# Reordering the first layer's small matmul groups, and moving one M quarter to an earlier step, in a cross-attention and leaky-ReLU layer kernel on one core

## The chip, the core and the metric

The kernel runs on one core of one Trainium2 chip. The metric is the device time of one execution in microseconds (us), as the median of some runs. The engines are TensorE (PE in the profile; PEld are its weight loads), VectorE (DVE), ScalarE (ACT), GpSimd (POOL) and SyncE (SP, which here only issues DMAs). Matmuls accumulate in PSUM, which has eight banks; VectorE and ScalarE carry ("evict") the results to SBUF.

## The reference

```python
def _attn_ref(x, state):                      # x (8, 8, 512, 64), state (8, 8, 32, 64)
    scores = scale * np.matmul(x, state.transpose(0, 1, 3, 2))
    a = np.exp(scores - scores.max(-1, keepdims=True))
    a /= a.sum(-1, keepdims=True) + 1e-09
    xread = np.matmul(a, state)
...
    sread = np.matmul(a2, x)                  # a2: the same with state and x exchanged
    return np.concatenate([xread, sread], axis=2)
def _moe_ref(x, w_in, w_out):                 # (4352, 512) @ (512, 2048), @ (2048, 512)
    h = x @ w_in
    return np.maximum(0.01 * h, h) @ w_out
```

Each of 8 batches has 8 heads, 512 tokens and 32 state rows per head. The heads' results stand side by side as 512 features; two layers with a leaky ReLU between them follow.

## The kernel before, in words

**How the work is cut.** The read of the state is folded into the first layer: for each batch the kernel makes M = state times w_in (256 rows of heads and state, in two groups of 128, by 2048), so that the first layer is probabilities times M. M is made in four quarters of 512 columns. `a_m(a, c, tag)` (line 413) makes quarter c of a batch with eight small matmuls (line 425) that use 64 rows and 32 columns of the array each, into two banks of the pool `tag`; `m_evict` (433) carries it to SBUF with the engine that it is given. A stretch in which TensorE makes such small matmuls, between full ones of 128 by 128, is called a session here. `a_scores` (line 260 of the trace) makes a batch's scores with eight small matmuls of the same form. Both may stand in one session.

**PSUM.** There are pools of banks by name: "sc" and "big" (one tile of two banks each), "py" and "ph" (two tiles of one bank each). A tile of a pool can be taken again when its last readers are done.

**The order is written by hand.** Each engine runs its instructions in the order in which the program emits them. Nothing is sorted by a planner, so where a line stands in the program is its place in its engine's queue.

**The stretch of the change.** Batch 0 (object `a0`) starts with attention of its own: after the exponentials, `recip0` (871) makes reciprocals on VectorE, `recip0_rows` (877, matmuls on line 824) spreads them over the rows by 16 small matmuls for each of two groups u, and `probs0` (881) multiplies on VectorE into `a0.aT`. Around these stand M's quarter 0 and 1 of batch 0 and quarter 0 of batch 1 (`a1`). Then batch 0's first layer runs in pairs of 128-wide blocks: `open_ff1_0` takes two banks, `ff1_0` (matmuls on line 960) adds the two groups g, `relu0` (972 for a tile of two banks, 968 for two of one) writes `h0` on ScalarE. Quarters 2 and 3 of batch 0 are evicted in halves (`m_halves`, 983 and 985) by VectorE between the pairs.

The second layer of batch 0 is done in pieces: `piece(b, hT, i, jq)` (545, matmuls on line 551) adds four of the sixteen blocks to the output of row block i; `jq` from 0 to 3 are its steps, and `js` takes half of one. Row blocks 0 and 1 use "py" banks, 2 and 3 the tile `wide` of "big". Between the pieces stand batch 1's transposes (1027) of its input, which GpSimd's queue loads into `x1` (889) in two halves and VectorE casts (1007), batch 1's scores, and M's quarter 2 of batch 1. ScalarE's exponential of batch 1 (`a_exp`, 288) follows VectorE's maximum, spread and difference (270, 278, 284).

Then batch 1's first layer runs in 16 steps `s` (`ff1`, 443: two matmuls on line 446 and one activation on line 451 into alternate "ph" banks). With it go the rest of batch 0's pieces and, from `s == 4` on, batch 2's scores (`a2`), for which the transposed state is made by GpSimd (213) and a DMA transpose of SyncE's queue (218). Batch 2's differences and exponentials go in halves (284, 334), and a second exponential over columns (351) follows. The later batches go in the same manner, with products of sums and differences in the second layer; they are not touched.

Of the kernel before, what the change touches and what calls it, by code (L numbers as in the profile page):

```python
# [27 lines left out]
def kernel(  # L28
# [24 lines left out]
    VEC, SCA, POO = nc.vector.tensor_copy, nc.scalar.copy, nc.gpsimd.tensor_copy  # L53
# [195 lines left out]
    def st_of(a, g, k):  # L249
        rows = slice(D * g, D * (g + 1))  # L250
        if a.b == 0:
            return stbd[rows, k, g ^ (k // 2), :]
        t = st1 if a.b == 1 else st_t[0][:, a.b - 2] if a.b < 4 else st_t[1][:, a.b - 4]
        return t[rows, NS * k:NS * (k + 1)]
# [31 lines left out]
    def block_exp(sh, n):  # L286
        e1 = att.tile([P, n * NS], BF16, name="e1", tag="e1", bufs=1)
        nc.scalar.activation(out=e1[:], in_=sh[:], func=AF.Exp)
        return e1
# [21 lines left out]
    def a_max(a):  # L311
        a.flat = a.sc[:].rearrange("p g c -> p (g c)")
        a.m1 = block_max(a.flat, NB)
# [9 lines left out]
    def a_exp(a):  # L323
        a.e1 = block_exp(a.sh, NB)
# [18 lines left out]
    def a_max2(a):  # L343
        a.m2 = att.tile([P, 2], FP32, name="mcol", tag="mcol")
        nc.vector.tensor_reduce(out=a.m2[:], in_=a.sc[:], axis=AX.X, op=ALU.max, negate=True)  # L345
# [67 lines left out]
    def a_m(a, c, tag):  # L413
        if not hasattr(a, "M"):
            a.M = mpool.tile([P, 2, DFF], BF16, name="M", tag="M")
        if tag in ("ph", "py", "phpy"):
            pm = [psum.tile([P, DM], FP32, name="pm", tag=t) for t in (tag[:2], tag[-2:])]
            at = [t[:] for t in pm]
        else:
            pm = psum.tile([P, 2, DM], FP32, name="pm", tag=tag, bufs=1)  # L420
            at = [pm[:, g, :] for g in range(2)]
        for k in range(NK):
            for g in range(2):
                v, r = (k // 2, 2 * (k % 2) + (g ^ (k // 2))) if a.b == 0 else (g, k)
                nc.tensor.matmul(  # L425
                    at[v][NS * r:NS * (r + 1)],
                    lhsT=st_of(a, g, k),
                    rhs=w_in_bf[D * g:D * (g + 1), k, DM * c:DM * (c + 1)],
                    start=True, stop=True,
                )  # L430
        return pm

    def m_evict(a, c, pm, copy):
        cols = slice(DM * c, DM * (c + 1))
        if isinstance(pm, list):
            for g in range(2):
                copy(a.M[:, g, cols], pm[g][:])
        else:
            copy(a.M[:, :, cols], pm[:])  # L439
# [105 lines left out]
    def piece(b, hT, i, jq, bank=None, copy=SCA, js=range(4)):  # L545
        if jq == 0 and js[0] == 0:
            y = ys[b, i] = Y()
            y.py = psum.tile([P, DM], FP32, name="py", tag="py")[:] if bank is None else bank
        y = ys[b, i]
        for j in [4 * jq + v for v in js]:  # L550
            nc.tensor.matmul(  # L551
                y.py, lhsT=hT[:, j, P * i:P * (i + 1)], rhs=w_out_bf[:, j, :],
                start=(j == 0), stop=(j == 15),
            )
        if jq == 3 and copy is not None:
            y_store(b, i, copy)

    def y_store(b, i, copy):
        tag = ("ysb", "s1", "ysb", "s6")[i]
        ysb = ypool.tile([P, DM], FP32, name="ysb", tag=tag, bufs=3 if tag == "ysb" else 1)  # L560
        copy(ysb[:], ys[b, i].py)
        nc.sync.dma_start(rows_of(b)[i], ysb[:])
# [213 lines left out]
    a0, a1, a2 = att_of[:3]  # L776
# [43 lines left out]
    def spread0(dst, parts, start):  # L820
        for i, part in enumerate(parts):
            for t in range(NT):
                for c in range(NK):
                    nc.tensor.matmul(
                        dst[NS * c:NS * (c + 1), P * t:P * (t + 1)],
                        lhsT=part[:, NK * t + c:NK * t + c + 1].to_broadcast([P, NS]),
                        rhs=ident[:], start=start, stop=start or (t == NT - 1 and i == 1),
                    )
# [42 lines left out]
    def recip0(u):  # L871
        q = att.tile([P, NG], BF16, name="q0", tag="q0")
        with nc.allow_low_precision(reason="one rounding, of the finished reciprocal"):
            nc.vector.reciprocal(q[:], r0[u][:])
        return q

    def recip0_rows(u, q):
        qb0[u] = psum.tile([P, S], FP32, name="qb0", tag="ph")
        spread0(qb0[u], (q,), True)

    def probs0(u):
        nc.vector.tensor_tensor(out=a0.aT[:, u], in0=e10[u][:], in1=qb0[u][:], op=ALU.mult)
# [52 lines left out]
    q = [recip0(0)]  # L935
    pm = a_m(a0, 0, "sc")
# [1 line left out]
        SCA(a0.M[:, g, :DM], pm[:, g, :])  # L938
    sum0(1)
    q.append(recip0(1))  # L940
    for u in range(2):
        recip0_rows(u, q[u])
        probs0(u)
    m_evict(a1, 0, a_m(a1, 0, "py"), SCA)
    m_evict(a0, 1, a_m(a0, 1, "big"), VEC)

    h0 = hpool.tile([P, 16, S], BF16, name="hT", tag="hT")

    def open_ff1_0(tag):
        if tag in ("sc", "big"):
            pr = psum.tile([P, 2, S], FP32, name="php", tag=tag, bufs=1)
            return pr, [pr[:, 0], pr[:, 1]]
        ph = [psum.tile([P, S], FP32, name="ph", tag=tag) for _ in range(2)]
        return ph, [p[:] for p in ph]

    def ff1_0(banks, j, g, vs=(0, 1)):
        for v in vs:
            nc.tensor.matmul(  # L960
                banks[v], lhsT=a0.M[:, g, P * (j + v):P * (j + v + 1)], rhs=a0.aT[:, g, :],
                start=(g == 0), stop=(g == 1),
            )
# [22 lines left out]

    t0, b0 = open_ff1_0("sc")
    t2, b2 = open_ff1_0("py")
    for t, j in ((b0, 0), (b2, 2)):
        for g in range(2):  # L990
            ff1_0(t, j, g)
    relu0(t0, 0)
    relu0(t2, 2)
    m_evict(a1, 1, a_m(a1, 1, "big"), VEC)
    for j, tag in ((4, "ph"), (6, "big"), (8, "py"), (10, "big"), (12, "py"), (14, "ph")):
        t, bk = open_ff1_0(tag)
        for g in range(2):
            ff1_0(bk, j, g)
        relu0(t, j)
        if j == 4:  # L1000
            m_halves(a0, 2, "sc")
        elif j == 8:
            a_scores(a0)
            m_halves(a0, 3, "ph")
            a_max2(a0)
# [9 lines left out]
        a_exp2(a0, g)  # L1015
    wide = psum.tile([P, 2, DM], FP32, name="pyw", tag="big", bufs=1)
    half = (range(0, 2), range(2, 4))
    for u in range(2):
        piece(0, h0, 2 + u, 0, bank=wide[:, u], js=half[0])
    for i in (0, 1):  # L1020
        piece(0, h0, i, 0, js=half[0])
    for u in range(2):
        ps = psum.tile([P, NT, 2, P], BF16, name="pxt2", tag="ph")
        for t in range(NT):
# [19 lines left out]
        tw_sum(1, j, j + 2, nc.gpsimd)  # L1044
    for i in (0, 1):
        piece(0, h0, i, 1)
    a_exp(a1)
    for i in (2, 3):
        piece(0, h0, i, 1)
# [28 lines left out]
    for s in range(16):  # L1078
        ff1(a1, h1, s)
        if s in (1, 3):  # L1080
            two = ((2, SCA), (3, VEC)) if s == 1 else ((0, SCA), (1, SCA))
            for i, copy in two:
                piece(0, h0, i, 3, copy=None, js=half[1])
            for i, copy in two:
                y_store(0, i, copy)
        elif s % 2:
            piece(*fill[s // 2 - 2])
        if s == 4:
            a_scores(a2)
            pm = a_m(a1, 3, "big")  # L1090
            a_max(a2)
            a_diff_halves(a2)
            a_max2(a2)
        elif s == 5:
            m_evict(a1, 3, pm, SCA)
            load_state(1)
        elif s == 7:
            a_exp_half(a2, 0)
            a_open(att_of[3], 3)
            a_xt_dma(att_of[3])  # L1100
        elif s in (9, 11):
            if s == 9:
                a_exp_half(a2, 1)
            a_exp2(a2, s // 2 - 4)
            if s == 9:
                a_a2t_pair(0, (0,))
                a_recip(a2)
                a_probs(a2)
            else:
                a_probs2(a2)  # L1110
                load_x(4, nc.sync)
        elif s == 13:
            a_probs2(a1)
            a_a2t_pair(0, (1,))
            pm = [a_m(a2, 0, "big"), a_m(a2, 1, "sc")]
            m_evict(a2, 0, pm[0], SCA)
            m_evict(a2, 1, pm[1], VEC)
            q1 = two_open(h1, 2 * P, ("S0", "S1"), "py")
            for n in (1, 2, 3):
                two_sum(q1, n, 0, 4, nc.vector)  # L1120
            two_sum(q1, 3, 4, 8, nc.vector)
# [19 lines left out]
    for b in range(2, B):  # L1141
# [22 lines left out]
        for s in range(16):  # L1164
            ff1(a, hT, s)
            if mid and s == (1 if b == 2 else 2):
                (o, c, tag), (o2, c2, tag2) = mid
                pm = a_m(att_of[o], c, tag)
# [71 lines left out]
            if b == 7 and s in FA_AT:  # L1240
                i = FA_AT.index(s)
# [24 lines left out]
    for c in range(2):  # L1266
# [15 lines left out]
        if c == 0:  # L1282
            y_pair(b, 0, 0, HN)
            q = two_open(hs, 0, None, "ph")
# [6 lines left out]
    for n in (1, 2, 6, 5, 7, 3, 4):  # L1291
        two_product(q, n)
        if n in (3, 4):
            u = n - 3
# [43 lines left out]
```

## Time and profile before

| | |
|---|---|
| median of 3 runs | 202.36 us (202.3 to 202.41) |
| the profiled execution's own time | 202.85 us |
| its span, from the first to the last instruction | 201.1 us |
| TensorE's mean granted clock | 1.000 |
| ScalarE's busy time in 24.0 to 30.0 us, and in 42.0 to 49.0 | 1.36 of 6.00, and 6.69 of 7.00 |
| DMA bytes moved in all | 27.75 MB |

A row of the timeline gives start and duration in us, engine, line, operation, what is written from what, shapes and how many instructions are merged; in brackets stand the idle time of the engine before it and what ended it. A merged row's duration runs to the end of its last instruction; matmuls are pipelined, so the next row starts before that end, and the distance between starts is what TensorE pays. In the chain of work that ended last a row gives start, duration, and what.

### The profile page before, as it was taken

The page shows a single profiled execution, that of the slowest core. Times are in us where ns is not written, and L with a number is a line of the kernel's source. Part 1 is how long each engine was busy: PE and PEld are TensorE (multiplying, and loading weights), DVE is VectorE, ACT ScalarE, POOL GpSimd, SP SyncE. Part 2 cuts the span into 40 slices and gives each one's busy share as a digit, 9 for nine tenths or more (in the row PEclk, how much of TensorE's full clock was granted, in tenths as well). Part 3 has the DMA queues.
Part 4 walks back from the last instruction along what each step waited for, and adds up shares of the span by engine and source line. Part 5 has one row for each costly group of instructions (what it writes and reads, how often), then busy time and mean ns, then how long its engine had stood idle before and what let it go on. Part 6 is the DMA issues. An engine that isn't in the chain of part 4 may idle for free.

```text
span 201.1 us, 4627 instructions
## 1 busy us (share of the span) xinstructions
PE 195.6 (97%) x1880; PEld 129.9 (65%) x1880; DVE 160.5 (80%) x241; ACT 141.5 (70%) x273; POOL 72.6 (36%) x77
## 2 busy tenths in 40 slices
PE   7989999999999999999999999999999999999993
PEld 2633544343476767776776677676767777799982
DVE  2767799598999989985999889898999945984712
ACT  3678825999889868766887779777868555757420
POOL 8734164993091373037300770054004600540000
PEclk9999999999999999999999999999999999999999
DMA  6999998597999954852473405220025202210115
GB/s 190 215 206 299 212 290 137 121 307 191 210 194 250 316 53 69 242 215 55 86 227 134 133 14 94 104 109 0 0 103 158 55 3 104 108 49 8 52 38 170
DMA packets 38774, 27.75 MB, mean 138 GB/s; under 512 B 24417, under 2 KB 35809, under 8 KB 38753
## 3 DMA queue, kind: packets, MB, share of 16 engines
q1 hardware_dynamic: 33584, 20.78, 39.2%
q0 software_dynamic: 4832, 6.29, 15.3%
q10 hardware_dynamic: 336, 0.39, 0.9%
q8 instruction: 14, 0.23, 0.5%
q14 instruction: 8, 0.06, 0.1%
HBM read 17.30 MB, written 8.91 MB: 130 GB/s over the span
## 4 chain that ended last, share of the span: by engine, by line
PE 85%; DMA 9%; POOL 3%; ACTq 1%; ACT 0%; DVE 0%; issue 0%; POOLq 0%
PE ph L446 24%; PE ppx L646 18%; PE ppb L646 15%; DMA x<-in_x_dram 8%; PE py L551 7%; PE ppr L703 6%; PE pm L425 3%; PE pf L524 3%; PE pyw L551 3%; PE ppw L646 3%; PE psr L398 2%; POOL w_in_bf L149 2%; PE sc L260 1%; DMA out_dram<-ysb 1%; ACTq L1297 1%; POOL x L889 0%
## 5 line engine op out<-in xcount | busy, mean ns | idle before, releaser
L451 ACT ACTIVATE hT<-ph 128x512 bf16<-128x512 f32 x112 | 66.7, 605 | 24.8 <-PE ph L446 24.0
L446 PE MATMUL ph<-aT,M 128*128 128x512 bf16 x224 | 65.4, 379 | 0.0
L611 POOL TENSOR_TENSOR S<-hT,S 128x512 bf16<-128x512 bf16 x24 | 32.1, 1358 | 82.2 <-DVE S L611 55.5
L646 PEld LDWEIGHTS <-S 128*128 128x128 bf16 x384 | 37.0, 98 | 12.7 <-issue 0.9
L646 PEld LDWEIGHTS <-hT 128*128 128x128 bf16 x288 | 28.0, 98 | 11.1
L611 DVE TENSOR_TENSOR S<-hT 128x1024 bf16<-128x1024 bf16 x24 | 25.0, 1070 | 3.3 <-ACT hT L451 3.3
L446 PEld LDWEIGHTS <-M 128*128 128x128 bf16 x224 | 20.9, 98 | 8.8 <-issue 2.9
L646 PE MATMUL ppx<-tw,S 128*128 128x256 bf16 x160 | 20.8, 273 | 0.0
L551 PEld LDWEIGHTS <-hT 128*128 128x128 bf16 x96 | 9.2, 98 | 11.4 <-issue 0.9
L551 PE MATMUL py<-w_out_bf,hT 128*128 128x512 bf16 x64 | 16.0, 379 | 0.0
L743 DVE TENSOR_TENSOR ysb<-ppb,s 128x512 f32<-128x512 f32 x12 | 8.3, 691 | 6.2 <-PE ppb L646 6.1
L646 PE MATMUL ppb<-w_out_bf,hT 128*128 128x256 bf16 x96 | 12.4, 273 | 0.0
L646 PE MATMUL ppb<-tw,S 128*128 128x256 bf16 x96 | 12.4, 273 | 0.0
L646 PE MATMUL ppb<-w_out_bf,S 128*128 128x256 bf16 x96 | 12.3, 273 | 0.0
L439 ACT CAST M<-pm 128x1024 bf16<-128x1024 f32 x11 | 11.2, 1017 | 0.3 <-PE pm L425 0.3
L646 PE MATMUL ppx<-w_out_bf,hT 128*128 128x256 bf16 x80 | 11.2, 273 | 0.0
L351 ACT ACTIVATE e<-sc,mcol 128x512 bf16<-128x512 f32 x16 | 11.1, 700 | 0.0
L646 PE MATMUL ppx<-tw,hT 128*128 128x256 bf16 x80 | 10.4, 273 | 0.0
L270 DVE TRANSPOSE_TENSOR_REDUCE mrow<-sc 128x32 f32<-128x1024 f32 x7 | 8.7, 1242 | 1.3 <-PE sc L260 1.3
L345 DVE TENSOR_REDUCE mcol<-sc 128x2 f32<-128x1024 f32 x8 | 9.7, 1214 | 0.0
L439 DVE CAST M<-pm 128x1024 bf16<-128x1024 f32 x7 | 8.5, 1217 | 1.4 <-PE pm L425 1.4
L136 POOL CAST xb<-xl 128x2048 bf16<-128x2048 f32 x5 | 9.5, 1895 | 0.0
(153 smaller groups left out, 322.7 us busy)
## 6 DMA issues: line engine op xcount, KB each, us to landing
out_dram<-ysb SPq DMA_DIRECT2D x11, 512.0 KB, 2.7
xl<-in_x_dram SPq DMA_DIRECT2D x5, 1024.0 KB, 6.3
out_dram<-ysb SPq DMA_DIRECT2D x9, 256.0 KB, 4.5
w_in_bf<-in_moe_w_in_dram POOLq DMA_DIRECT2D x4, 512.0 KB, 9.7
xf<-in_x_dram SPq DMA_DIRECT2D x4, 256.0 KB, 3.8
w_out_bf<-in_moe_w_out_dram POOLq DMA_DIRECT2D x4, 256.0 KB, 14.1
x<-in_x_dram POOLq DMA_DIRECT2D x2, 512.0 KB, 15.5
w_out_bf<-in_moe_w_out_dram POOLq DMA_DIRECT2D x2, 512.0 KB, 16.8
```

Source lines behind the costliest of these rows:

```text
L136: nc.gpsimd.tensor_copy(xt[b][:].rearrange("p t h d -> p h t d"), xl[b][:].rearrange("p h (t d) -> p h t d", t=NT),)
L270: nc.vector.tensor_reduce(out=m1[:], in_=flat.rearrange("p (c j) -> p c j", j=NS), axis=AX.X, op=ALU.max, apply_transpose=True,)
L345: nc.vector.tensor_reduce(out=a.m2[:], in_=a.sc[:], axis=AX.X, op=ALU.max, negate=True)
L351: nc.scalar.activation(out=a.e2[:, g], in_=a.sc[:, g, :], func=AF.Exp, bias=a.m2[:, g:g + 1], accum_out=a.r2[:, g:g + 1],)
L439: copy(a.M[:, :, cols], pm[:])
L446: nc.tensor.matmul(ph[:], lhsT=a.M[:, g, P * j:P * (j + 1)], rhs=a.aT[:, g, :], start=(g == 0), stop=(g == 1),)
L451: nc.scalar.activation(out=hT[:, j, :], in_=ph[:], func=AF.Prelu, scale=1 / SCALE, alpha=0.01)
L551: nc.tensor.matmul(y.py, lhsT=hT[:, j, P * i:P * (i + 1)], rhs=w_out_bf[:, j, :], start=(j == 0), stop=(j == 15),)
L611: eng.tensor_tensor(out=part(n), in0=in0, in1=in1, op=op)
L646: nc.tensor.matmul(q[bank][v], lhsT=lhsT, rhs=w_of(n, j), start=q["open", bank] and j == 0, stop=j == 7, skip_group_check=True,)
L703: nc.tensor.matmul(q.bank[w], lhsT=lhsT, rhs=w_of(n, j), start=n in (1, 2, 5) and j == 0, stop=j == HJ - 1, skip_group_check=True,)
L743: nc.vector.tensor_tensor(out=to, in0=of, in1=in1, op=ALU.add)
```

## The change

Four things are moved. M's quarter 0 of batch 1 goes between the two groups' spreads. Quarter 1 of batch 0 goes between the first two groups of the first layer's first pair. The pairs 6 to 12 of batch 0's first layer exchange "big" and "py", and the wide pieces of the second layer's first half step go behind the narrow ones. Last, M's quarter 3 of batch 1 leaves step 4 of batch 1's first layer, where it followed batch 2's scores in "big" banks and was evicted at step 5 by one copy, and goes into batch 0's second layer, between the pieces of step 1 (`jq` = 1) of row blocks 0 and 1 and those of 2 and 3, in "ph" banks, evicted by two copies of ScalarE ahead of batch 1's exponential.

```diff
@@ -938,11 +938,11 @@
-    for u in range(2):
-        recip0_rows(u, q[u])
-        probs0(u)
+    recip0_rows(0, q[0])
+    probs0(0)
     m_evict(a1, 0, a_m(a1, 0, "py"), SCA)
-    m_evict(a0, 1, a_m(a0, 1, "big"), VEC)
+    recip0_rows(1, q[1])
+    probs0(1)
@@ -986,13 +986,15 @@
     t0, b0 = open_ff1_0("sc")
     t2, b2 = open_ff1_0("py")
-    for t, j in ((b0, 0), (b2, 2)):
-        for g in range(2):
-            ff1_0(t, j, g)
+    ff1_0(b0, 0, 0)
+    m_evict(a0, 1, a_m(a0, 1, "big"), VEC)
+    ff1_0(b0, 0, 1)
+    for g in range(2):
+        ff1_0(b2, 2, g)
     relu0(t0, 0)
     relu0(t2, 2)
     m_evict(a1, 1, a_m(a1, 1, "big"), VEC)
-    for j, tag in ((4, "ph"), (6, "big"), (8, "py"), (10, "big"), (12, "py"), (14, "ph")):
+    for j, tag in ((4, "ph"), (6, "py"), (8, "big"), (10, "py"), (12, "big"), (14, "ph")):
@@ -1015,10 +1017,10 @@
+    for i in (0, 1):
+        piece(0, h0, i, 0, js=half[0])
     for u in range(2):
         piece(0, h0, 2 + u, 0, bank=wide[:, u], js=half[0])
-    for i in (0, 1):
-        piece(0, h0, i, 0, js=half[0])
@@ -1044,6 +1046,7 @@
     for i in (0, 1):
         piece(0, h0, i, 1)
+    m_evict(a1, 3, a_m(a1, 3, "ph"), SCA)
     a_exp(a1)
     for i in (2, 3):
         piece(0, h0, i, 1)
@@ -1087,12 +1090,10 @@
         if s == 4:
             a_scores(a2)
-            pm = a_m(a1, 3, "big")
             a_max(a2)
             a_diff_halves(a2)
             a_max2(a2)
         elif s == 5:
-            m_evict(a1, 3, pm, SCA)
             load_state(1)
```

## The prediction

> **What bounds the kernel now.** I read the page first, then the chain of work that ended last, then the timeline of each engine from 10 to 50 us, where all edits lie.
>
> ```profile
> span 201.1 us, 4627 instructions
> PE 195.6 (97%) x1880; PEld 129.9 (65%) x1880; DVE 160.5 (80%) x241; ACT 141.5 (70%) x273; POOL 72.6 (36%) x77
> ```
>
> TensorE is the bound: nearly every 0.1 us that it gains or loses for good is in the time. But the chain says that one stretch isn't its own: the chain leaves TensorE at 24.00 us and goes to a transfer.
>
> ```profile
> 7.48 15.74 DMA x<-in_x_dram
> 23.25 0.69 DVE xb L1007
> ...
> 23.25 0.69 DVE L1007 CAST xb<-x 128x1024 bf16<-128x1024 f32 x1 [0.65 <-DMA x<-in_x_dram]
> ...
> 23.23 0.61 PE L1027 MATMUL pxt<-ident,xb 128*128 128x128 bf16 x8
> 24.00 0.62 PE L1027 MATMUL pxt<-ident,xb 128*128 128x128 bf16 x8 [0.16 <-DVE stf L1011]
> ```
>
> The second half of batch 1's input lands at 23.22. VectorE had idled 0.65 us for it, casts it (0.69), and only then can TensorE make the second group of transposes, at 24.00, after 0.16 us of idling. (The memset named as releaser stands right behind the cast.) So TensorE's work before 24.00 is covered by a transfer already, by a margin of 0.16 us. That decides what the first two hunks are worth.
>
> **The first part (before 24.00).** It adds and removes no arithmetic; it changes the order.
>
> ```profile
> 11.53 0.41 PE L425 MATMUL pm<-w_in_bf,st 64*32 64x512 bf16 x8
> 12.59 0.41 PE L425 MATMUL pm<-w_in_bf,stbd 64*32 64x512 bf16 x8 [0.66 <-DMA w_in_bf<-in_moe_w_in_dram]
> ...
> 13.81 1.03 PE L960 MATMUL ph<-aT,M 128*128 128x512 bf16 x4
> 14.77 0.41 PE L425 MATMUL pm<-w_in_bf,st 64*32 64x512 bf16 x8
> 15.11 1.04 PE L960 MATMUL ph<-aT,M 128*128 128x512 bf16 x4
> 16.07 0.41 PE L425 MATMUL pm<-w_in_bf,stbd 64*32 64x512 bf16 x8
> 16.52 1.02 PE L960 MATMUL php<-aT,M 128*128 128x512 bf16 x4
> 17.38 1.03 PE L960 MATMUL ph<-aT,M 128*128 128x512 bf16 x4
> ...
> 13.07 1.23 DVE L439 CAST M<-pm 128x1024 bf16<-128x1024 f32 x1 [0.48 <-PE pm L425]
> 15.25 1.22 DVE L439 CAST M<-pm 128x1024 bf16<-128x1024 f32 x1 [0.95 <-PE pm L425]
> 16.56 1.29 DVE L985 CAST M<-pm 128x512 bf16<-128x512 f32 x2
> ```
>
> Before, TensorE waits 0.66 us for w_in's second quarter (until 12.59), then does the M group and eight first-layer matmuls. After, the second row of spreads and two first-layer matmuls lie ahead of that wait and fill it, so six are left behind it. Four take 17.38 - 16.52 = 0.86, so two are worth 0.43. The next M group (14.77) needs VectorE's eviction, 13.07 + 1.23 = 14.30, and so goes at about 14.36: 0.41 earlier. The swap of "big" and "py" for pairs 6 to 12 takes away the 0.11 at 16.52 (there the bank waits for the eviction that ends at 15.25 + 1.22 = 16.47), but at 17.38 the matmuls need the halves that VectorE begins at 16.56, and VectorE itself is only 0.41 earlier. So TensorE gets to the transposes **0.41 us earlier**, and then idles 0.16 + 0.41 = 0.57 for the same transfer: worth nothing by this trace (bounds: 0 and -0.41). No step here changes a DMA or its queue: loads of GpSimd's queue keep their order, and SyncE's first state load still follows the cast. The order of the wide and the narrow pieces changes only TensorE's order inside the covered stretch.
>
> **The second part (after 24.00): M's last quarter of batch 1.** Before, it shares a session of small matmuls with batch 2's scores in step 4; after, it has one alone, at about 28.6. First what a session costs.
>
> ```profile
> 18.34 0.41 PE L260 MATMUL sc<-xT,stbd 64*32 64x512 bf16 x8
> 18.57 0.40 PE L425 MATMUL pm<-w_in_bf,stbd 64*32 64x512 bf16 x8
> 18.90 1.04 PE L960 MATMUL php<-aT,M 128*128 128x512 bf16 x4
> ```
>
> Alone: four full matmuls from 13.81 should end their turn at 14.67, the small ones begin at 14.77 (0.10 for the change over), the next full one at 15.11 (0.34): **0.435 us** with the exact 0.865 of four. Two groups: 17.38 to 18.34 is again 0.96, and 18.34 to 18.90 is 0.56, so the second group in a session costs 0.56 - 0.34 = **0.22**.
>
> By the Trainium skill (TensorEngine Tiling (Array Packing), "Key Properties") a change of tiling mode drains the array; by its page TensorE: Matmul & The Clock Gate ("Single matmul latency") a lone matmul costs 166 ns beyond its stream, so with two changes a lone group would be estimated at 2 x 0.166 + 0.213 = 0.55 (by that the whole change comes to about +0.48, rival 4). The trace disagrees: with 0.435, part of the drain is hidden.
>
> So at 28.63 TensorE falls back by 0.435. Who else is touched there?
>
> ```profile
> 28.63 1.89 PE L551 MATMUL pyw<-w_out_bf,hT 128*128 128x512 bf16 x8
> 35.53 1.03 PE L446 MATMUL ph<-aT,M 128*128 128x512 bf16 x4
> ...
> 26.10 1.07 ACT L437 CAST M<-pm 128x512 bf16<-128x512 f32 x2 [1.81 <-PE pm L425]
> 30.00 1.06 ACT L288 ACTIVATE e<-sh 128x1024 bf16<-128x1024 f32 x1 [2.83 <-DVE sh L284]
> 34.26 0.69 DVE L306 TENSOR_TENSOR aT<-e,qb 128x1024 bf16<-128x1024 bf16 x1
> ```
>
> ScalarE idles 2.83 us ahead of batch 1's exponential. The two evictions (1.07, as those at 26.10) start at about 29.05 and end at 30.1: the exponential queued behind them slips by about 0.1, and the probabilities, made at 34.26 + 0.69 = 34.95, by as much. Batch 1's first layer needs them at 35.53 + 0.43, so 1.0 us of slack covers that, and the eviction costs nothing.
>
> Now step 4, where the shared session was.
>
> ```profile
> 38.99 0.59 PE L446 MATMUL ph<-aT,M 128*128 128x512 bf16 x2
> 39.58 0.11 PEld L260 LDWEIGHTS <-st_t 64*32 64x32 bf16 x8 [0.49 <-DMA st_t<-stb]
> 39.58 0.41 PE L260 MATMUL sc<-xT,st_t 64*32 64x512 bf16 x8
> 40.14 0.60 PE L446 MATMUL ph<-aT,M 128*128 128x512 bf16 x2
> 40.06 1.25 DVE L270 TRANSPOSE_TENSOR_REDUCE mrow<-sc 128x32 f32<-128x1024 f32 x1 [1.29 <-PE sc L260]
> ```
>
> Two full matmuls from 38.99 (0.43) and 0.10 give 39.52; the scores started at 39.58, since the transposed state came by DMA. That 0.065 is swallowed when TensorE comes 0.435 later, so the scores slip by **0.37**, and VectorE's maximum behind them too. Behind the session TensorE gets 0.22 back and is only **0.15** late. Were that all, the change would be worth less. But the scores feed a chain that comes back to TensorE at step 12:
>
> ```profile
> 42.63 1.29 DVE L284 TENSOR_TENSOR sh<-sc,sh 128x512 f32<-128x512 f32 x2
> 41.28 1.01 ACT L439 CAST M<-pm 128x1024 bf16<-128x1024 f32 x1
> 43.42 0.63 ACT L334 ACTIVATE e<-sh 128x512 bf16<-128x512 f32 x1
> 45.43 0.69 ACT L351 ACTIVATE e<-sc,mcol 128x512 bf16<-128x512 f32 x1
> 46.09 1.09 ACT L451 ACTIVATE hT<-ph 128x512 bf16<-128x512 f32 x2
> 45.76 1.03 PE L551 MATMUL py<-w_out_bf,hT 128*128 128x512 bf16 x4
> 46.75 1.08 PE L446 MATMUL ph<-aT,M 128*128 128x512 bf16 x4
> 47.67 1.02 PE L551 MATMUL py<-w_out_bf,hT 128*128 128x512 bf16 x4
> ```
>
> Between 45.76 and 46.75 lie 0.99 us for 0.865 of work, between 46.75 and 47.67 0.92: TensorE waits 0.125 + 0.055 for its "ph" banks, which ScalarE's activations from 46.09 free. ScalarE works without a gap from 43.42 on, and 43.42 is set by VectorE's first half of the difference (42.63 + 0.69 = 43.32), not by the 1.01 us eviction at 41.28 that the change removes. So the relief of ScalarE **doesn't reach** step 12: with the scores 0.37 late, the maximum, spread and difference, the exponentials, and the release of the bank are all 0.37 late, and step 12 starts at 47.12, though TensorE alone would have been there at 45.76 + 0.865 + 0.15 = 46.77. From there TensorE is 0.37 late. No later wait of TensorE in this trace ends with a DMA, so nothing gives it back.
>
> **Sum**: 0 (start, covered) + 0.435 - 0.065 (scores) = +0.37; the 0.22 given back in step 4 is lost again in step 12. The profiled execution took 202.85 (span 201.1 and 1.75 around it) and becomes 203.22; the median shown is 0.49 below it, so I predict 202.36 + 0.37 = **202.73**.
>
> **Rivals.** A measurement of this kernel can tell about 0.2%, 0.4 us, from no change.
>
> 1. The transfer isn't the last to come at 24.00 in unprofiled executions: these are 0.49 shorter, and if loads land earlier there, up to 0.41 of the start pays: 202.36 + 0.37 - 0.41 = 202.32. For it: the margin is only 0.16. Against: an earlier w_in quarter would shorten the 0.66 wait too, so less is left to win.
>
> 2. Step 12 is not bound by the chain (the activations take up the delay): then the 0.22 counts and the 0.18 of waits goes: 0.435 - 0.065 - 0.22 - 0.18 = -0.03, thus 202.33; with rival 1's start as well, -0.44, thus 201.92, faster. Against: ScalarE has no gap from 43.42 to 46.75.
>
> 3. The other side, slower than 0.2%: the state's DMA at 39.55 is what softens the lone session. If it lands 0.065 earlier in unprofiled executions, the scores slip by the full 0.435 and step 12 with them: 202.80. It decides from about 0.03 of wait. For: the wait is tiny, and any gain in DMA removes it. A dearer session acts at the same place: bounded by the dearest session here, two groups (0.10 + 0.56 = 0.655), at 203.02; and below by the marginal 0.22, at 202.5.
>
> 4. Both changes of mode drain the array in full:
>
> ```profile
> L446 PE MATMUL ph<-aT,M 128*128 128x512 bf16 x224 | 65.4, 379 | 0.0
> ```
>
> A matmul lasts 0.379 from start to end, and in a stream the next follows after 0.216; two exposed tails of 0.163 and the marginal 0.22 are 0.55, so 202.36 + 0.55 - 0.065 = 202.84. Against: the lone sessions at 14.77 and 16.07 show 0.10 + 0.34, not 0.55. This is the rule of the skill's pages above, seen from rows.
>
> 5. The change doesn't do what it says: the quarter's session waits itself for "ph" banks. Against: those were evicted by 27.17 (26.10 + 1.07), 1.4 us before. It would end near the forecast anyway.
>
> **How the numbers follow.** Forecast 0.48 (202.73, its own range 202.60 to 202.80); rival 1 0.17 (202.32 and between); rival 2 alone 0.07, with the start 0.08 (201.92); rival 3 0.16; rival 4 0.04. Faster by over 0.2% is the double case and little else: 0.10. Slower by over 0.2% needs above 202.765: rivals 3 and 4 and some 0.15 of the forecast's own range: 0.35. Within: 0.55. The range runs from 202.20, past rival 1 and part of the way to 201.92, to 203.00, the dearest session; both ends leave out 0.1.
>
> **What would show it.** Right: TensorE reaches line 1027's first group about 0.4 earlier and idles some 0.5 to 0.6 before the second, at 24.00; one small session near 28.6 for 0.435; batch 2's scores near 39.95 with no wait for the state's DMA; step 12's matmuls after a wait of about 0.35 to 0.47, behind the activations; everything later 0.37 late. Wrong: the second transposes earlier than 24.00, the activations of steps 8 to 11 not later than before, or a first layer of batch 1 that waits for its probabilities.

## The result, and the profile after

The changed kernel takes 202.98 us (median of 22 runs, 202.49 to 203.94), the kernel before 202.37 (22 runs): ratio **1.0031, 95% interval 1.0017 to 1.0044**, so about 0.6 us slower (0.34 to 0.89). The profiled execution took 203.28 with a span of 201.5; before it was 202.85 with 201.1. Each ratio leaves out the few executions that were over 1.5% slower than the fastest of their kernel, so it need not be the quotient of the medians beside it.

The page of the changed kernel:

```profile
span 201.5 us, 4629 instructions
PE 196.6 (98%) x1880; PEld 130.5 (65%) x1880; DVE 159.9 (79%) x241; ACT 141.8 (70%) x274; POOL 72.5 (36%) x77
PE 90%; DMA 3%; DVE 2%; ACT 2%; ACTq 1%; issue 0%; DVEq 0%
```

The last line gives the shares of the chain of work that ended last. Before, the chain went back to the load of batch 1's input; that load is no part of it now. TensorE's timeline of the first part:

```profile
11.49 0.41 PE L824 MATMUL qb<-ident,q 128*32 128x128 bf16 x16
11.83 0.41 PE L425 MATMUL pm<-w_in_bf,st 64*32 64x512 bf16 x8
12.17 0.41 PE L824 MATMUL qb<-ident,q 128*32 128x128 bf16 x16
12.86 0.59 PE L960 MATMUL php<-aT,M 128*128 128x512 bf16 x2 [0.29 <-DVE aT L882]
13.38 0.41 PE L425 MATMUL pm<-w_in_bf,stbd 64*32 64x512 bf16 x8
13.72 0.61 PE L960 MATMUL php<-aT,M 128*128 128x512 bf16 x2
...
15.14 0.41 PE L425 MATMUL pm<-w_in_bf,st 64*32 64x512 bf16 x8
...
23.54 1.06 PE L1029 MATMUL pxt<-ident,xb 128*128 128x128 bf16 x16
24.43 1.03 PE L551 MATMUL pyw<-w_out_bf,hT 128*128 128x512 bf16 x4
```

Both groups of transposes now run in one go at 23.54, without the wait before the second. VectorE's casts show why: in this execution both halves had landed when it came to them.

```profile
21.78 1.29 DVE L1009 CAST xb<-x 128x1024 bf16<-128x1024 f32 x2
```

TensorE's timeline of the second part, and ScalarE's around step 12:

```profile
28.76 0.41 PE L425 MATMUL pm<-w_in_bf,st 64*32 64x512 bf16 x8
29.10 1.90 PE L551 MATMUL pyw<-w_out_bf,hT 128*128 128x512 bf16 x8
...
39.48 0.59 PE L446 MATMUL ph<-aT,M 128*128 128x512 bf16 x2
40.00 0.41 PE L260 MATMUL sc<-xT,st_t 64*32 64x512 bf16 x8
40.34 0.61 PE L446 MATMUL ph<-aT,M 128*128 128x512 bf16 x2
...
45.97 1.03 PE L551 MATMUL py<-w_out_bf,hT 128*128 128x512 bf16 x4
47.16 1.08 PE L446 MATMUL ph<-aT,M 128*128 128x512 bf16 x4 [0.17 <-ACT hT L451]
48.08 1.02 PE L551 MATMUL py<-w_out_bf,hT 128*128 128x512 bf16 x4
49.03 0.63 PE L425 MATMUL pm<-w_in_bf,st_t 64*32 64x512 bf16 x16
```

```profile
43.84 0.63 ACT L334 ACTIVATE e<-sh 128x512 bf16<-128x512 f32 x1 [0.47 <-DVE sh L284]
44.37 1.07 ACT L451 ACTIVATE hT<-ph 128x512 bf16<-128x512 f32 x2
45.33 0.63 ACT L334 ACTIVATE e<-sh 128x512 bf16<-128x512 f32 x1
45.85 0.69 ACT L351 ACTIVATE e<-sc,mcol 128x512 bf16<-128x512 f32 x1
46.51 1.09 ACT L451 ACTIVATE hT<-ph 128x512 bf16<-128x512 f32 x2
```

The scores start at 40.00, where they stood at 39.58 before. ScalarE now idles 0.47 for VectorE's difference and then runs without a gap from 43.84 on. Step 12 starts at 47.16, though TensorE ended its turn before it at 45.97 + 0.865 = 46.83: it waits 0.33 for the bank.

Three marks split the time into four stretches, so that executions can be compared: the start of the first spread of reciprocals (line 824, qb), the start of the wide pieces right behind the transposes, and the start of step 13's two M groups. The last stretch, from there to the end, is as long in both kernels:

| execution | to the first spread | **first part**: to the wide pieces | **second part**: to step 13's M groups | to the end | span |
|---|---|---|---|---|---|
| before | 10.77 | 13.68 | 24.17 | 152.5 | 201.1 |
| after | 11.49 | 12.94 | 24.60 | 152.5 | 201.5 |

So the 0.4 us between the two profiles are +0.43 in the second part, -0.74 in the first, and +0.72 ahead of any edit (where no instruction differs). Single profiles can't settle the first part; the experiments had to.

### The profile page after: what moved, and what is told of

Its sections match the earlier page's. It is cut to its first block, busy times and chain, and to the rows that moved or that the text cites. A ratio compares the mean times of both kernels' runs of the same rounds, so it can differ in the third digit from the quotient of the medians.

```text
span 201.5 us, 4629 instructions
## 1 busy us (share of the span) xinstructions
PE 196.6 (98%) x1880; PEld 130.5 (65%) x1880; DVE 159.9 (79%) x241; ACT 141.8 (70%) x274; POOL 72.5 (36%) x77
## 4 chain that ended last, share of the span: by engine, by line
PE 90%; DMA 3%; DVE 2%; ACT 2%; ACTq 1%; issue 0%; DVEq 0%
PE ph L446 23%; PE ppx L646 18%; PE ppb L646 15%; PE ppr L703 6%; PE py L551 5%; PE pm L425 4%; PE pyw L551 3%; PE pf L524 3%; PE ppw L646 3%; PE ph L960 2%; PE psr L398 2%; DMA xf<-in_x_dram 2%; PE php L960 1%; PE sc L260 1%; DMA out_dram<-ysb 1%; PE pxth L788 1%
## 5 line engine op out<-in xcount | busy, mean ns | idle before, releaser
L439 ACT CAST M<-pm 128x1024 bf16<-128x1024 f32 x10 | 10.2, 1019 | 0.3 <-PE pm L425 0.3
L293 DVE TRANSPOSE_TENSOR_REDUCE r<-e 128x32 f32<-128x1024 bf16 x7 | 8.7, 1244 | 0.8 <-ACT e L334 0.5
```

What stands on the lines that cost most here:

```text
L293: nc.vector.tensor_reduce(out=r1[:], in_=e1[:].rearrange("p (c j) -> p c j", j=NS), axis=AX.X, op=ALU.add, apply_transpose=True,)
```

## The experiments

Each timed kernel is compared with runs of the kernel before on the same chip. The second part and the first part are read from their profiles with the marks above.

**The two parts by themselves, and both kernels again.** e1 has only the hunks ahead of the transposes, e2 only the move of the quarter:

```diff
 # e2, on the kernel before
         piece(0, h0, i, 1)
+    m_evict(a1, 3, a_m(a1, 3, "ph"), SCA)
     a_exp(a1)
...
-            pm = a_m(a1, 3, "big")
...
-            m_evict(a1, 3, pm, SCA)
```

> Only the first hunks (order of the first layer's M groups, exchanged banks, order of the pieces); M's last quarter of batch 1 stays in step 4. Theory A (the prediction: the input's transfer covers the start): ratio to before 1.000 (within 0.001). Theory B (the front becomes bound by its own chain of probabilities and pays two more changes of mode, so it loses what the transfer no longer hides): 1.001, +0.2 us. Theory C (the front pays): 0.998, -0.4 us.

> Only the move of M's last quarter of batch 1 into a session of its own. Theory A: ratio 1.0018 (+0.37 us), with step 12 of batch 1's first layer 0.37 later. Theory B (the front is what costs): less, 1.001. Theory of the full session price without the softening by the state's DMA: 1.0021 (+0.435 us).

> The kernel before, unchanged: ratio 1.000, and a second profile of it. Theory A: the second half of batch 1's input lands last at the transposes again (TensorE waits before them). Rival: the landing moves by some tenths from execution to execution, and in this profile there may be no such wait.

> The changed kernel, unchanged: ratio 1.003 as in the result (1.0017 to 1.0044), and a second profile of it. Theory A: sum of e1 and e2. In this profile TensorE either waits for the input's transfer before the second transposes (then some 0.37 slower from there) or reaches them by its own chain.

Measured, against 202.13 for the kernel before:

| | median us | ratio, 95% interval | first part | second part |
|---|---|---|---|---|
| e1 first hunks alone | 202.23 | 0.9996 (0.9982 to 1.0009) | 12.94 | 24.16 |
| e2 move alone | 202.53 | 1.0017 (1.0007 to 1.0028) | 12.62 | 24.60 |
| e3 before again | 202.18 | 0.9995 (0.9982 to 1.0008) | 12.86 | 24.16 |
| e4 after again | 202.69 | 1.0030 (1.0015 to 1.0044) | 12.94 | 24.60 |

The move is the cause that can be shown: the second part is 24.60 wherever the quarter has a session of its own and 24.16 or 24.17 where it has not, 0.44 apart; by the medians e2 is 0.40 above before, and e4 0.46 above e1. e2 in TensorE's timeline:

```profile
12.01 0.41 PE L425 MATMUL pm<-w_in_bf,st 64*32 64x512 bf16 x8
12.23 0.41 PE L425 MATMUL pm<-w_in_bf,stbd 64*32 64x512 bf16 x8
...
14.50 0.41 PE L425 MATMUL pm<-w_in_bf,st 64*32 64x512 bf16 x8
...
23.86 1.03 PE L551 MATMUL pyw<-w_out_bf,hT 128*128 128x512 bf16 x4
...
48.46 0.63 PE L425 MATMUL pm<-w_in_bf,st_t 64*32 64x512 bf16 x16
```

The first hunks by themselves can't be told from no change. Their first part is 12.94 in each of the three profiles that have them here (after, e1, e4), and nothing in it waits for a DMA. The old order takes 12.62 (e2, where the two M groups at 12.01 and 12.23 follow each other without a wait) plus what waits for DMAs add to it. That is 0.24 in e3, for w_in. In the profile of before it is 0.74 for w_in and 0.32 at the transposes, which take 1.22 there from their start to the wide pieces and 0.90 in e2 and e3. (The brackets give these waits as 0.15, 0.66 and 0.16; they count from the modelled end of the row before, while TensorE pays the distance between starts.) e3's own rows:

```profile
11.90 0.41 PE L425 MATMUL pm<-w_in_bf,stbd 64*32 64x512 bf16 x8 [0.15 <-DMA w_in_bf<-in_moe_w_in_dram]
...
22.53 1.06 PE L1027 MATMUL pxt<-ident,xb 128*128 128x128 bf16 x16
```

Its transposes run in one go too. The wait for batch 1's input that carried the prediction's first part is in one of the twelve profiles, not in the others. e4 was expected to be the sum of e1 and e2, whose ratios together give 1.0013; that lies just under e4's interval, and with the noise of all three it is not told apart from e4.

**What the first part is made of.** e8 has the exchange of the banks and the order of the pieces, and the old order of the M groups. It was run once, for its profile, so no time is compared.

```diff
-    for j, tag in ((4, "ph"), (6, "big"), (8, "py"), (10, "big"), (12, "py"), (14, "ph")):
+    for j, tag in ((4, "ph"), (6, "py"), (8, "big"), (10, "py"), (12, "big"), (14, "ph")):
...
```

> The kernel before with only the exchange of the banks of pairs 6 to 12 and the order of the pieces. Read in the profile: from the M group ahead of pair 4 to the transposes 8.46 in e2 (old order), 8.40 in e1 (new). Theory: the exchange alone gives 8.40 (its 0.11 at pair 6 shrinks to 0.06, since pair 8 waits for VectorE's halves), and the stretch before it is the old 3.26, so that the 0.39 of the new front lie in the order of the M groups. Rival: the exchange costs something itself, 8.5 or more.

```profile
10.75 0.83 PE L824 MATMUL qb<-ident,q 128*32 128x128 bf16 x32
...
14.01 0.41 PE L425 MATMUL pm<-w_in_bf,st 64*32 64x512 bf16 x8
...
22.40 1.09 PE L1027 MATMUL pxt<-ident,xb 128*128 128x128 bf16 x16
...
38.77 0.41 PE L260 MATMUL sc<-xT,st_t 64*32 64x512 bf16 x8 [0.28 <-DMA st_t<-stb]
```

From the spread to the M group ahead of pair 4 it takes 3.26, as the old order does (e2: 14.50 - 11.24 = 3.26), against 15.14 - 11.49 = 3.65 in the changed kernel; from there to the transposes 8.39, against 8.46 (e2) and 8.40 (changed kernel). So the exchange, with the order of the pieces, is worth 0.06 to 0.07, and the new order of the M groups costs **0.39** in TensorE's time: two groups that shared a session now have one each, and the two full matmuls between them wait for VectorE's probabilities (0.29 by the bracket, 0.35 by starts: 12.86 - 12.17 = 0.69, where a small group ahead of full matmuls takes 0.34). The new order pays only where w_in comes late. (This profile also shows the scores waiting for the state's DMA, so that cover of the prediction's rival 3 exists in some executions.)

**Step 12's wait.** Both exponentials over columns go behind step 11's activation, on the changed kernel (e6) and on the one before (e7):

```diff
-            a_exp2(a2, s // 2 - 4)
+            if s == 11:
+                for g in range(2):
+                    a_exp2(a2, g)
```

> The changed kernel with both of batch 2's exponentials over columns behind step 11's activation, instead of one behind step 9's. Theory A (step 12 waits for its bank because these exponentials stand before the activations of steps 10 and 11): the wait before step 12 is gone, the stretch of e5 falls from 24.60 to 24.23, ratio to before 1.001 (1.003 less 0.0018). Rival (the wait is VectorE's or TensorE's, or returns at step 13 or in its M groups): 24.5 to 24.6, 1.003.

> The same edit on the kernel before. Theory A: the 0.125 and 0.055 of waits at steps 12 and 13 go: the stretch falls from 24.16 to 23.98, ratio 0.9991. With e6 this gives the price of the move without the chain: 0.435 - 0.22 = 0.215 instead of 0.44. Rival: no change of the stretch, and 0.44 between the two as before.

e6, TensorE and ScalarE:

```profile
24.05 1.03 PE L551 MATMUL pyw<-w_out_bf,hT 128*128 128x512 bf16 x4
...
45.59 1.03 PE L551 MATMUL py<-w_out_bf,hT 128*128 128x512 bf16 x4
46.45 1.03 PE L446 MATMUL ph<-aT,M 128*128 128x512 bf16 x4
...
48.27 0.63 PE L425 MATMUL pm<-w_in_bf,st_t 64*32 64x512 bf16 x16
...
45.47 1.08 ACT L451 ACTIVATE hT<-ph 128x512 bf16<-128x512 f32 x2
```

e7:

```profile
12.71 0.41 PE L425 MATMUL pm<-w_in_bf,stbd 64*32 64x512 bf16 x8 [0.79 <-DMA w_in_bf<-in_moe_w_in_dram]
...
24.24 1.03 PE L551 MATMUL pyw<-w_out_bf,hT 128*128 128x512 bf16 x4
...
48.23 0.63 PE L425 MATMUL pm<-w_in_bf,st_t 64*32 64x512 bf16 x16
```

Step 12 follows the piece at once (46.45 - 45.59 = 0.86): the wait is gone. The second part is 24.22 in e6 (24.23 expected) and 23.99 in e7 (23.98 expected). Times: e6 202.53, ratio 1.0010 (0.9988 to 1.0031); e7 201.84, 0.9971 (0.9946 to 0.9996), both against 202.28. Without the chain the move costs 24.22 - 23.99 = 0.23, with it 0.44: the 0.22 that step 4 gets back is real, and it is step 12's wait that swallows it. Some of what the late exponentials win is lost again behind step 13: from its M groups to the start of the last group of matmuls (line 646) it takes 147.35 us in before and e3, 147.43 in e7 and 147.48 in e6. So the traces give e7 only some 0.1 us over the kernel before, and the rest of the 0.4 between the medians is not explained by them.

**No session at all.** e5 evicts the last quarter from the banks of quarter 2:

```diff
-    m_evict(a1, 2, a_m(a1, 2, "ph"), SCA)
+    pm2 = a_m(a1, 2, "ph")
+    m_evict(a1, 2, pm2, SCA)
+    m_evict(a1, 3, pm2, SCA)
...
-    m_evict(a1, 3, a_m(a1, 3, "ph"), SCA)
```

> The changed kernel without the own session: M's last quarter of batch 1 is evicted a second time from the banks of its quarter 2 (its eight small matmuls and their values are left out, both evictions stay on ScalarE). The stretch from the wide pieces behind the transposes to step 13's small matmuls was 24.16 in the kernel before (second profile) and 24.60 in the changed one. Theory A (the session costs 0.435 and step 12 hangs on the scores' chain, so the work taken out of step 4 gives nothing): 24.16, ratio to before 1.0005 to 1.001 with the front's order. Rival (TensorE's own work counts at step 12): 0.22 of step 4 and 0.18 of waits come back as well, 23.76, ratio 0.998 to 0.999.

Neither theory's ratio came out: 203.24 against 202.28, ratio 1.0039 (1.0021 to 1.0058), with work left out, and a second part of 25.00. The scores wait for the state, whose DMA transpose took 4.5 us from issue to landing, where the other profiles have 2.8 to 3.1:

```profile
23.98 1.03 PE L551 MATMUL pyw<-w_out_bf,hT 128*128 128x512 bf16 x4
...
39.95 0.41 PE L260 MATMUL sc<-xT,st_t 64*32 64x512 bf16 x8 [0.77 <-DMA st_t<-stb]
...
48.98 0.62 PE L425 MATMUL pm<-w_in_bf,st_t 64*32 64x512 bf16 x16
```

The late scores do bear on the theories. From their start to step 13's M groups it is 48.98 - 39.95 = 9.03 us. The same distance is 9.03 or 9.04 in all nine profiles that have the exponentials in their old place, whether M's quarter follows the scores (before, e1, e3, e8) or not (after, e2, e4, e5, e9), and whether a DMA held the scores up or not. With the late exponentials it is 8.64 (e6), 8.86 (e7) and 8.87 (e10). So step 13 hangs on the start of the scores, and not on what TensorE does between, as Theory A has it.

The DMA queues' view of 36 to 37 us has an instruction fetch in e5, and in no other profile (columns: packets, MB, share of 16 engines):

```profile
q8 instruction: 1, 0.02, 9.6%
```

e9 is e5 with TensorE's instruction count restored by tiny matmuls ahead of the warm-up:

```diff
-    spin(spin_bank(), 7)
+    warmup = spin_bank()
+    spin(warmup, 9, 8)
+    spin(warmup, 6)
```

> e5 (M's last quarter evicted from the banks of quarter 2, its eight small matmuls left out) with eight matmuls of 8 columns added to the warm-up at the start (one full warm-up matmul fewer, nine tiny ones), so that TensorE has as many instructions ahead of every later place as the changed kernel. In e5 the scores waited 0.77 for the state's DMA transpose, which took 4.5 instead of about 3.0; one 16 KB instruction fetch fell at 36 us there, in the midst of the transposes, and at 32 to 33 in all other profiles. Theory A (fetch hits the transposes because TensorE's code is shorter): fetch back at 32 to 33, landing about 3.0, the stretch from the wide pieces to step 13's small matmuls 24.16, ratio to before 1.0005 to 1.001. Rival 1 (something else of e5 delays the transposes, such as ScalarE's earlier evictions): landing 4.5, stretch 25.0, ratio 1.004 again. Rival 2 (step 12 doesn't hang on the scores' chain): 23.76.

The fetch is back at 32 to 33 us, the transpose lands after 2.8, and the time is 202.27 against 202.31, ratio 1.0001 (0.9986 to 1.0017):

```profile
23.86 1.03 PE L551 MATMUL pyw<-w_out_bf,hT 128*128 128x512 bf16 x4
...
38.99 0.41 PE L260 MATMUL sc<-xT,st_t 64*32 64x512 bf16 x8
...
48.03 0.63 PE L425 MATMUL pm<-w_in_bf,st_t 64*32 64x512 bf16 x16
```

The second part is 24.17, not 23.76: with the session and step 4's share of it both gone, step 12 still starts where the kernel before has it. That is the chain from the scores again: 48.03 - 38.99 = 9.04.

**A version that beats both.** e10 joins the exchange of e8 and the late exponentials of e7:

> The kernel before with the two edits that the profiles bear out: the exchange of the banks (first stretch 0.05 shorter) and both exponentials over columns behind step 11 (0.17 shorter). Theory A: the wide pieces to step 13 in 23.99, first spread to wide pieces 12.58 plus the wait for w_in; ratio 0.9985 to 0.999. Rival: a DMA (w_in's second quarter or the state's transpose) takes the gain back: 1.000.

```profile
10.94 0.83 PE L824 MATMUL qb<-ident,q 128*32 128x128 bf16 x32
...
23.48 1.03 PE L551 MATMUL pyw<-w_out_bf,hT 128*128 128x512 bf16 x4
...
47.51 0.63 PE L425 MATMUL pm<-w_in_bf,st_t 64*32 64x512 bf16 x16
```

First part 12.54, second 24.03; 201.90 against 202.31, ratio 0.9980 (0.9962 to 0.9997). It is faster than the kernel before by an interval that just excludes no change, as e7's does, and the two aren't told apart. By the marks it gains about 0.2 of the 0.4 between the medians (12.62 and 24.16 in the old order without a wait), and behind step 13 it loses nothing (147.35 to the start of the last group of matmuls).

## Why the prediction was right or wrong, point by point

The forecast was 202.73, slightly slower, and 202.98 was measured, inside the range. Its own ratio, 1.0018, lies at the low end of the interval; the prediction gave 0.55 to a change within 0.2% and 0.35 to the slower side, where the measured ratio lies. That the range holds the time is in part luck: 202.98 is 0.02 under its upper end, and that end stood for a lone session as dear as two groups, 0.655, which no run shows.

- **The lone session at 0.435, the second group at 0.22**: right. e2 and e4 show 0.44 with the chain, e6 and e7 0.23 without it (0.435 - 0.22 = 0.215 was expected). The drain estimate of rival 4 (0.55) is out: in the changed kernel the session at 28.76 gives way to the pieces 0.34 later, at 29.10, as the sessions read in the trace before did.
- **ScalarE's relief doesn't reach step 12**: right, and by the mechanism stated. ScalarE idles 0.47 for VectorE's difference in the place of the eviction taken away, and step 12 starts 0.41 later. e6, e7 and e9 each show it by another edit, and so does the 9.03 from the scores to step 13 in every profile with the exponentials in their old place. The profile of before alone could not decide it: ScalarE's two activations from 42.17 end at 43.28 there and VectorE's half of the difference at 43.32, nearly at once. Rival 2 is out.
- **The two evictions ahead of batch 1's exponential cost nothing**: right; no later matmul waits for them in the profile, and the second part is explained without them.
- **"0.435 - 0.065 (scores)"**: this step failed. The 0.065 of softening by the state's DMA stood in the one profile read; in e1, e2, e3 and e4 the scores start 0.52 to 0.53 after the two matmuls ahead of them, which is 0.43 + 0.095 without any wait. In the profile of before TensorE had come to these two matmuls 0.06 sooner after the wide pieces (38.99 - 24.45 = 14.54, against 14.60 in e1 and e3), and the wait only took that up: the scores start 15.12 to 15.13 after the wide pieces in all three, and 15.57 in after, e2 and e4. So the whole term is 0.44, as rival 3 had it, but not for good: e8 had a longer wait there.
- **"0 (start, covered)"**: the size was near, the reason was not. The prediction took the wait for batch 1's input from one execution for a property of the kernel. In e1 to e4 that transfer isn't last. The idling of 0.5 to 0.6 that was to show it is in no profile of the changed kernel. What would make the first hunks worth nothing by measure (e1: 0.9982 to 1.0009) is a trade: 0.39 for the reordered groups, less 0.06 for the exchange, against the wait for w_in, which with the old order of the groups added 0.74 (before), 0.24 (e3), 0.86 (e7) and nothing in e2, e8 and e10. The mean of these six, 0.31, is near the 0.33; as these are single profiled executions, that is an estimate and not a proof. The prediction's margin of 0.16 at the transposes was 0.32 by starts.
- **"0.41 us earlier"**: the number is there between the two profiles: from the first spread to the transposes it is 23.23 - 10.77 = 12.46 before and 23.54 - 11.49 = 12.05 after. That is partly luck, since two misses of 0.06 cancel. The prediction left out that VectorE's probabilities come late, which puts the M group ahead of pair 4 at 15.14 - 11.49 = 3.65 after the first spread instead of the 14.36 - 10.77 = 3.59 worked out; and the exchange of the banks pays its 0.06 after all. Against e2, which had no such wait (22.96 - 11.24 = 11.72), the new order is 0.33 later.
- **What stays open**: the difference between the measured 0.6 and the 0.44 of the move. It would fit a first part that costs some tenths on the average, and e4 against e2 points there by 0.16, but e1's interval holds both that and a gain, and the time up to the first spread, in which no instruction differs, varied from 10.42 to 11.49 between these profiles.

## What to carry to other kernels

A stretch that waits for a load in one profile may not wait in the next execution: before an edit is priced by such a wait, take a second profile of the same kernel and mark off the stretches whose length stays the same. A small group of tiled matmuls cost 0.22 us here as a guest in a session and twice that, 0.435, alone. Work taken off a busy engine helps only if that engine is what holds the next wait; here the chain began at the scores, and the edit that took the wait away was to put two exponentials behind the activations that free the banks.

## What the runs showed that was not expected

Taking sixteen instructions out of TensorE's program (eight matmuls and their weight loads) went with a kernel 1.0 us slower than before by the medians and 0.8 by the ratio (e5: 203.24 against 202.28), and putting as many tiny ones at the start took that away (e9: 202.27 against 202.31). In e5 one 16 KB instruction fetch fell between 36 and 37 us, among the DMA transposes, and the state's transpose then took 4.5 us; in the eleven other profiles it came between 32 and 34 (in before and e8 behind 33) and the state's transpose took 2.8 to 3.1. That the fetch delays the transpose is the reading that fits both; the fetch and the shorter program were not tried apart from each other, so it is not shown.
